# Block 0's attention head sums through DRAM, a later output projection, and block 1's sums behind LN2

## The chip, the cores and the metric

The kernel runs on one core of one Trainium2 chip. The metric is the device time of one execution in microseconds (us); the median of several executions is quoted. One profiled execution gives the trace, whose span is about 2 us shorter than that time. Every variant was run beside the kernel before, on the same chip in the same rounds. Where two variants are compared with each other, they can be from different rounds; the medians of the kernel before differ by at most 0.4 us between rounds (1617.8 to 1618.2).

## The reference

Two transformer layer pairs, A then B, applied twice to x of 2048 tokens by 1024 features in bf16. A is a sliding-window attention with 32 heads of 32 features, 8 offsets per token at distance 2; B is a gated ReLU MLP of 3584 hidden features.

```python
x = A_x
x = x + _A_ref(_layernorm(x), A_wqkv, A_wo)
x = x + _B_ref(_layernorm(x), B_W_gate, B_W_up, B_W_down)
x = x + _A_ref(_layernorm(x), A_wqkv, A_wo)
x = x + _B_ref(_layernorm(x), B_W_gate, B_W_up, B_W_down)
# _A_ref: logits[h, s, w] = sum over the head's 32 features of q[s] * k[s - 2w], masked where s < 2w,
#         softmax over the 8 offsets w, o = attn @ shifted v, then o @ wo
# _B_ref: (relu(x @ W_gate) * (x @ W_up)) @ W_down
```

## The kernel before

The kernel works in 4 token blocks of 512, twice, as n = 0 to 7. It is one list of timed events (`ev`): every event has a nominal time, and the list is sorted by it. TensorE, VectorE and the SP queue are chained to that order (point 3), and the times only set the order. Four parts matter here.

1. *Attention of a block on VectorE.* `prod_sum_steps` multiplies q by shifted k and sums over eight chunks of features, in two halves of the offsets (h = 0, 1), into a tile `s`. What is left of a head is then spread over four partitions, and those four rows have to be added (the "head sums"). Softmax and P·V (`pv_steps`) follow, the result goes to DRAM and comes back transposed as `oT` for the output projection `wo`.
2. *Head sums.* For block 0 before the change, TensorE adds the four rows by a multiplication with a 0/1 matrix `sel`. For all other blocks the tile goes out to DRAM and comes back regrouped, and VectorE adds.

```python
def head_mm(n):                      # block 0, before
    st["L"] = psum_l.tile([P, W, P], F32, tag="L")
    for wh in range(2):
        for tq in range(TPB):        # 8 matmuls
            mm(st["L"][32*tq:32*tq+32, WH*wh:WH*(wh+1), :], lhsT=sel[:],
               rhs=st["s"][:, tq, WH*wh:WH*(wh+1), :], ...)

def head_sum(n):                     # other blocks
    s4 = att[n].pop("s4")            # loaded back from DRAM by load_s
    u = work.tile([P, DG // 2, W, P], F32, tag="ac", bufs=1)
    dv(nc.vector.tensor_tensor, u[:], s4[:, 0:2], s4[:, 2:4], op=ALU.add)
    dv(nc.vector.tensor_tensor, u[:, 0], u[:, 0], u[:, 1], op=ALU.add)
```

3. *The chains of order.* `dv` puts every VectorE instruction behind the one before, and `sp_dma` does the same for transfers on the SP queue. On ScalarE the exponential of the softmax is put behind the instruction listed before it, but the casts of V are put behind nothing, so later casts can run ahead of it. An instruction that has to wait holds up all that were listed after it on that engine or queue.

```python
def sp_dma(dst, src, transpose=False):
    with tc.issue_after(tail_sp[0]):
        tail_sp[0] = start(dst, src).ins
```

4. *Weights.* They come in slabs of 1 MB through a ring of five buffers, as SP transfers in the same queue. The gate and up weights of the MLP are cut into slabs of four 128-column chunks; "slab 4" holds chunks 16 to 19. The MLP of block 0 starts at `t_gu0` with alternating gate and up groups of 8 matmuls; VectorE multiplies relu(gate) by up into `hT`.

The events around block 0's attention, before (cut):

```python
ahead = 2 * KC + 6                   # q/k groups of blocks 2, 3 ahead of wo of block 0 (22 of 32)
t_wo0 = t_qk2 + GRP * ahead
t_fill = t_wo0 + GRP * KC
t_gu0 = t_fill + GRP * (4 * KC - ahead)
...
ev.append((t_v2 + 5.2 * GRP, lambda: head_mm(0)))
spread(softmax_steps(0), t_v2 + 5.3 * GRP, 0.01)
spread(pv_steps(0), t_pv0, 4.3)
...
sums1 = prod_sum_steps(1)            # 16 steps, about 30 VectorE operations
spread(sums1[:4], t_pv0 + 34.5, 4.5)
spread(sums1[4:6], t_wo0 + 0.5, 2.5)
spread(sums1[6:10], t_fill + 1.4, 4.6)
spread(sums1[10:], t_gu0 + 2.6, 5.4)
...                                  # in the MLP of block 0, at = t_gu0:
ev.append((at + 4.0, store_s(1, 0)))
ev.append((at + 37.5, store_s(1, 1)))
ev.append((at + 40.5, load_s(1)))
```

## Time and profile before

| | before |
|---|---|
| time, median | 1618.2 us |
| span of the profiled run | 1616.1 us |
| TensorE busy / VectorE busy | 99% / 70% |
| TensorE waits in all | 2.6 us, all in the first 11 us |
| granted TensorE clock | 1.000 |
| one group of 8 matmuls (128x512) | 1.727 us from start to start |

TensorE is the limit. First come the page's line of busy times, then, from its part on the chain that ended last, the shares by engine.

```profile
PE 1607.6 (99%) x7584; PEld 786.4 (49%) x7633; DVE 1138.5 (70%) x962; ACT 473.5 (29%) x964; POOL 180.3 (11%) x168
...
PE 99%; issue 0%; DMA 0%; DVE 0%; POOL 0%; ACT 0%; DVEq 0%
```

The page says what is busy, but not how near each stage is to a hole. That has to be read from the timelines. Here is VectorE's timeline of the kernel before, around block 0's attention. Columns: start, duration, engine, line, operation, output<-inputs, count, and in brackets the idle time before it and what ended it.

```profile
100.09 2.29 DVE L106 TENSOR_TENSOR s<-ac,t 128x2048 bf16<-128x2048 f32 x1
103.78 0.27 DVE L106 TENSOR_TENSOR L<-L,maskc 32x112 f32<-32x112 f32 x1 [1.40 <-PE L L132]
104.09 1.23 DVE L106 TENSOR_REDUCE m<-L 128x128 f32<-128x1024 f32 x1
...
111.88 4.50 DVE L106 TENSOR_TENSOR pv<-a,vhm 128x4096 bf16<-128x4096 bf16 x2
```

And here is SP's queue of the same kernel, in the MLP of block 0. The columns are the same; the duration is that of the issue, not of the transfer.

```profile
218.29 0.53 SPq L121 DMA_DIRECT2D q<-q_d  x1
230.40 0.56 SPq L121 DMA_DIRECT2D s_d<-s  x1
...
233.84 2.52 SPq L121 DMA_DIRECT2D s<-s_d  x4
...
237.09 1.67 SPq L121 DMA_DIRECT2D w_u<-in_B_W_up_dram  x1
```

The sums of block 0 end at 102.4; TensorE's head sums are there at 103.8, and P·V begins at 111.9. The sums of block 1 end at 230.4 (VectorE's last of them starts at 228.08 and takes 2.29 us). SP's store of them (`s_d<-s`) was reached at 218.8 and had to wait until then; behind it in the queue stand the loads of the sums and then the up weights of slab 4 (`w_u`, 237.09). These weights took 9.4 us to land, at 246.5, and TensorE's first group with them begins 33 groups after 190.01, at 247.0. Its timeline has wo of block 0, the first gate group and that up group at:

```profile
158.93 13.98 PE L132 MATMUL acc_wo<-w_o,oT 128*128 128x512 bf16 x62
...
190.01 1.89 PE L132 MATMUL acc_g<-xnT_b,w_g 128*128 128x512 bf16 x8
...
246.99 1.89 PE L132 MATMUL acc_u<-xnT_b,w_u 128*128 128x512 bf16 x8
```

### The profile page before, as it was taken

The page shows a single profiled execution, that of the slowest core. Times are in us where ns is not written, and L with a number is a line of the kernel's source. Part 1 is how long each engine was busy: PE and PEld are TensorE (multiplying, and loading weights), DVE is VectorE, ACT ScalarE, POOL GpSimd, SP SyncE. Part 2 cuts the span into 40 slices and gives each one's busy share as a digit, 9 for nine tenths or more (in the row PEclk, how much of TensorE's full clock was granted, in tenths as well). Part 3 has the DMA queues.
Part 4 walks back from the last instruction along what each step waited for, and adds up shares of the span by engine and source line. Part 5 has one row for each costly group of instructions (what it writes and reads, how often), then busy time and mean ns, then how long its engine had stood idle before and what let it go on. Part 6 is the DMA issues. An engine that isn't in the chain of part 4 may idle for free.

```text
span 1616.1 us, 18879 instructions
## 1 busy us (share of the span) xinstructions
PE 1607.6 (99%) x7584; PEld 786.4 (49%) x7633; DVE 1138.5 (70%) x962; ACT 473.5 (29%) x964; POOL 180.3 (11%) x168
## 2 busy tenths in 40 slices
PE   9999999999999999999999999999999999999999
PEld 6646544444444445444454444544445444444444
DVE  5999989996989698929389293893939939311211
ACT  4753312132115313603136031361313311131110
POOL 3400100010003002300053000530005100000000
PEclk9999999999999999999999999999999999999999
DMA  9767857596669666784747847489575884655452
GB/s 308 181 187 247 219 163 255 183 218 203 208 195 227 191 185 208 194 248 145 227 159 203 237 156 226 156 202 255 163 227 155 207 241 157 209 161 177 156 167 67
DMA packets 359064, 317.92 MB, mean 197 GB/s; under 512 B 105024, under 2 KB 332736, under 8 KB 358464
## 3 DMA queue, kind: packets, MB, share of 16 engines
q1 hardware_dynamic: 358272, 315.87, 67.1%
q8 instruction: 59, 0.97, 0.3%
q10 hardware_dynamic: 704, 0.85, 0.2%
q14 instruction: 29, 0.24, 0.0%
HBM read 266.29 MB, written 34.66 MB: 186 GB/s over the span
## 4 chain that ended last, share of the span: by engine, by line
PE 99%; issue 0%; DMA 0%; DVE 0%; POOL 0%; ACT 0%; DVEq 0%
PE acc_u L132 24%; PE acc_g L132 24%; PE dacc L132 18%; PE acc_v L132 7%; PE acc_k L132 7%; PE acc_q L132 7%; PE acc_wo L132 7%; PE dacc_pair L132 6%; DMA x<-in_A_x_dram 0%; PE tp_pair L384 0%; DVE bst L103 0%; DVE bst L106 0%; POOL rstd L327 0%; PE L L132 0%; DVE x L838 0%
## 5 line engine op out<-in xcount | busy, mean ns | idle before, releaser
L132 PE MATMUL acc_u<-xnT_b,w_u 128*128 128x512 bf16 x1792 | 423.3, 379 | 0.0
L132 PE MATMUL acc_g<-xnT_b,w_g 128*128 128x512 bf16 x1792 | 423.3, 379 | 0.0
L791 ACT ACTIVATE r<-acc_g 128x512 bf16<-128x512 f32 x224 | 133.6, 596 | 727.5 <-PE acc_g L132 696.8
L106 DVE TENSOR_TENSOR hT<-acc_u,r 128x512 bf16<-128x512 f32 x224 | 150.6, 685 | 241.2 <-PE acc_u L132 238.5
L132 PE MATMUL dacc<-w_d,hT 128*128 128x512 bf16 (+1 forms) x1372 | 300.4, 375 | 1.5
L132 PEld LDWEIGHTS <-hT 128*128 128x128 bf16 x1820 | 178.0, 98 | 209.0
L132 PEld LDWEIGHTS <-w_u 128*128 128x128 bf16 x1792 | 175.3, 98 | 211.4
L132 PEld LDWEIGHTS <-w_g 128*128 128x128 bf16 x1792 | 175.4, 98 | 211.4
L106 DVE TENSOR_TENSOR pv<-a,vhm 128x4096 bf16<-128x4096 bf16 x64 | 143.5, 2282 | 0.0
L838 DVE TENSOR_TENSOR x<-dacc,x 128x512 bf16<-128x512 f32 (+1 forms) x38 | 24.5, 672 | 154.2 <-PE dacc L132 154.2
L606 DVE TENSOR_TENSOR t<-q,k 128x2048 f32<-128x2048 bf16 x56 | 128.0, 2292 | 6.7 <-ACT k L541 4.6
L106 DVE TENSOR_TENSOR t<-q,k 128x2048 f32<-128x2048 bf16 x56 | 127.4, 2285 | 3.7 <-ACT k L541 2.6
L106 DVE TENSOR_TENSOR pv<-pv 128x1024 bf16<-128x1024 bf16 (+1 forms) x128 | 113.7, 949 | 0.0
L547 POOL COPY kh<-k 128x14 bf16<-128x14 bf16 x40 | 56.0, 1406 | 504.2 <-ACT k L541 504.2
L132 PE MATMUL acc_wo<-w_o,oT 128*128 128x512 bf16 x498 | 111.1, 379 | 0.7
L622 DVE TENSOR_TENSOR ac<-ac,t 128x2048 f32<-128x2048 f32 x48 | 109.6, 2284 | 0.3
L106 DVE TENSOR_TENSOR ac<-ac,t 128x2048 f32<-128x2048 f32 x48 | 109.6, 2283 | 0.0
L263 POOL TENSOR_TENSOR st_b<-st_b,neg_half 128x1 f32<-128x1 f32 x29 | 43.9, 1521 | 525.8 <-ACT st_b L262 525.8
L132 PE MATMUL dacc_pair<-w_d,hT 128*128 128x512 bf16 x413 | 95.5, 379 | 0.4
L132 PEld LDWEIGHTS <-oT 128*128 128x128 bf16 x512 | 50.2, 98 | 60.3
L258 ACT ACTIVATE xn_b<-x 128x1024 bf16<-128x1024 bf16 x29 | 30.3, 1045 | 129.3 <-DVE x L106 67.1
L444 ACT CAST vT<-acc_v 128x512 bf16<-128x512 f32 x56 | 32.6, 585 | 57.0 <-PE acc_v L132 56.1
(134 smaller groups left out, 1227.2 us busy)
## 6 DMA issues: line engine op xcount, KB each, us to landing
w_g<-in_B_W_gate_dram SPq DMA_DIRECT2D x56, 1024.0 KB, 7.1
w_u<-in_B_W_up_dram SPq DMA_DIRECT2D x56, 1024.0 KB, 5.4
w_d<-in_B_W_down_dram SPq DMA_DIRECT2D x48, 1024.0 KB, 5.9
w_o<-in_A_wo_dram SPq DMA_DIRECT2D x16, 1024.0 KB, 8.2
vhm<-v_d SPq DMA_DIRECT2D x32, 284.0 KB, 6.7
v_d<-vT SPq DMA_DIRECT2D x8, 1024.0 KB, 9.7
oT<-o_d SPq DMA_DIRECT2D x32, 256.0 KB, 3.4
w_d<-in_B_W_down_dram SPq DMA_DIRECT2D x16, 512.0 KB, 3.9
```

Source lines behind the costliest of these rows:

```text
L106: tail_dve[0] = f(*args, **kwargs).ins
L132: tail_pe[0] = nc.tensor.matmul(*args, **kwargs).ins
L258: nc.scalar.activation(xn, xt[:], ACT.Square, accum_out=sq)
L263: nc.gpsimd.tensor_tensor(rstd, vpe, neg_half[:, 0:1], op=ALU.pow)
L444: tail_act[0] = nc.scalar.copy(st["vT"][:, c, :], acc[:]).ins
L547: nc.gpsimd.tensor_copy(khalo[n][:, c, :], k[:, BLK:BLK + HALO])
L606: nc.vector.tensor_tensor(t[:], i0, i1, op=ALU.mult)
L622: nc.vector.tensor_tensor(o, i0, i1, op=ALU.add)
L791: tail_act[0] = nc.scalar.activation(rs[j][:], acc[:], ACT.Relu).ins
L838: run = dv if n < NB - 2 else (lambda f, *args, **kwargs: f(*args, **kwargs))
```

## The change

Its intent: take block 0's head sums off the busiest engine as in the other blocks, and make room for the longer way: wo of block 0 comes two groups later, and block 1's sums no longer stand between wo's results and LN2. The diff, cut to its core:

```diff
-    sel = const.tile([P, H], BF16, name="sel")        # and its construction, and head_mm
-    def load_s(n):
+    def load_s(n, w0=0, w1=W):                         # a range of offsets
+            s4 = work.tile([P, DG, w1 - w0, P], BF16, tag="t", ...)
-    def head_sum(n):
+    def head_sum(n, w0=0, w1=W):
+        lo, hi = (st["u"][:, i, w0:w1, :] for i in range(2))
+        dv(nc.vector.tensor_tensor, st["u"][:, :, w0:w1, :], s4[:, 0:2], s4[:, 2:4], op=ALU.add)
+        dv(nc.vector.tensor_tensor, lo, lo, hi, op=ALU.add)
         def shift():
-            Lt = st["L"][:] if n == 0 else head_sum(n)
+            if n == 0:
+                head_sum(n, 0, WH)
+                head_sum(n, WH, W)
+            else:
+                head_sum(n)
+            Lt = st.pop("u")[:, 0]
-    ahead = 2 * KC + 6
+    ahead = 3 * KC
+    ev.append((t_sum0 + 4.4 * KC + 1.5, store_s(0, 0)))
+    ev.append((t_sum0 + 4.4 * (2 * KC - 1) + 0.1, store_s(0, 1)))
+    ev.append((t_sum0 + 4.4 * (2 * KC - 1) + 0.2, load_s(0, 0, WH)))
+    ev.append((t_sum0 + 4.4 * (2 * KC - 1) + 0.3, load_s(0, WH, W)))
-    ev.append((t_v2 + 5.2 * GRP, lambda: head_mm(0)))
-    t_pv0 = t_v2 + 4.2 * GRP + 10.0
+    t_pv0 = t_v2 + 4.2 * GRP + 15.0
-    spread(sums1[:4], t_pv0 + 34.5, 4.5)
-    spread(sums1[4:6], t_wo0 + 0.5, 2.5)
-    spread(sums1[6:10], t_fill + 1.4, 4.6)
-    spread(sums1[10:], t_gu0 + 2.6, 5.4)
+    spread(sums1[:4], t_pv0 + 34.5, 3.2)
+    spread(sums1[4:9], t_fill + 3.3, 3.0)
+    spread(sums1[9:], t_gu0 + 2.6, 5.4)
```

Below, part 1 is the way through DRAM, part 2 the later wo (`ahead`), part 3 the new order of `sums1`.

## The prediction

> **What bounds the kernel now.** TensorE. The chain of waits is 99% PE; the list of waits shows PE waiting 2.6 us in all, within the first 11 us. PE's timeline has no gap from 17 us on: 8 matmuls every 1.727 us. So the change can gain only what it takes off PE, and loses every new hole it opens.
>
> **Removed.** The 8 head-sum matmuls. In the timeline they push the next group from 103.03 (by the 1.727 us pitch) to 103.66: -0.63 us. wo of block 0 only changes places with two k groups.
>
> **Added, on VectorE.** Block 0's sums end at 102.38; its softmax started at 103.78. Now: store of the second half (block 1's took 3.4 us; here 1 MB of V is still leaving), four loads issued 0.45 us apart, each landing in 2.7 to 4 us: there at about 110.5. Then 1.9 us of adds (scaled from block 1's 2.28 + 1.22), and the maximum from SBUF costs 1.90 instead of 1.23 from PSUM. P·V starts about 121 instead of 111.88: VectorE is 9 to 10 us late, with almost no idle time until 230 to absorb it.
>
> **Critical path, step by step.**
> 1. wo of block 0 starts at 161.8. P·V ends about 155.5, store 2.3, first load 2.7: oT just in time; hole 0 to 1 us.
> 2. LN2 of block 0 has no sums in its middle any more, so its transposes land by about 187: no hole before the first gate group.
> 3. Those sums now stand ahead of the first gate product: 11 operations x 2.24 us after LN2's end (182.5) put it at 207 instead of 201.2. With six accumulators and three r buffers, gate j must finish before up-group j+4. Hole of 2 to 4 us near 205.
> 4. The largest: the second half of block 1's sums ends about 241.5 instead of 230.37 (9.3 chain, 0.6 LN2 wait, two more gate products ahead). The store of those sums blocks the SP queue until then (waits of SP: 11.6 us for s), and behind it come the s loads and the up-weights of slab 4. Before, that weight load was issued at 237.09 and landed at 246.5; PE needs it at 190.01 + 33 x 1.727 = 247.0: slack 0.5 us. It lands 16.1 us after the sums end, so now at about 257.6. PE is then 10.6 us late in all, step 3 included.
> 5. After it VectorE and PE are both about 11 us late, so their distance is as before: no further hole.
>
> The Trainium skill, "DMA: Bandwidth & Descriptors", section on the anatomy of one DMA, says that a semaphore wait is served by the issuing sequencer before dispatch, not by the DMA engines. This trace agrees: SP issues nothing between 218.8 and 230.4 us. So an unrelated weight load suffers.
>
> **Predicted:** 1618.0 + 10.6 = 1628.6 us; 80% range 1620.5 to 1635. Chances: faster by over 2% 0.01, within 2% 0.97, slower 0.02.
>
> **What would show it.** Step 1: P·V from about 121, PE waiting under 1 us for oT. Step 3: PE waits for hT near 205. Step 4: SP waiting about 20 us for s until 241.5; PE idle 6 to 10 us near 250, ended by a DMA of w_u. Step 5: no PE wait over 1 us after 260. Removed matmuls: groups after 103 are 0.63 us earlier.
>
> **What would make it wrong.** If the half loads land by 107, the hole of step 4 shrinks us for us. If the weight load, issued later, lands faster than 9.4 us, the hole is up to 4 us smaller. If PSUM buffers are assigned otherwise, step 3 grows, but step 4 swallows that. If all holes close, the time is 1617.4.

## The result

The changed kernel took 1639.0 us (1638.0 to 1639.5, four runs) against 1618.2 us of the kernel before in the same rounds: ratio 1.0128, interval 1.011 to 1.0145. It is slower by 20.8 us, within the 2% that counts as the same, but far outside the noise. The profiled run took 1638.0 us, the fastest of the four, so its trace holds about 1 us less than the medians say.

The changed kernel's page has the same outline, with PE at 91% of the chain instead of 99% (the page's busy line, then the chain's shares by engine), although busy time on PE is again 99%:

```profile
PE 1612.0 (99%) x7576; PEld 787.1 (48%) x7625; DVE 1143.4 (70%) x966; ACT 473.1 (29%) x964; POOL 178.0 (11%) x165
...
PE 91%; DVE 5%; DMA 2%; issue 1%; SPq 0%; POOL 0%; ACT 0%; DVEq 0%; POOLq 0%
```

The list of TensorE's waits of the changed kernel shows three that were not there (columns: line that waited <- releaser: us in total, times, longest). Before, the list held none of these lines, only waits of 1.5, 0.8 and 0.3 us at the start of the program.

```profile
PE acc_u L132 <- DMA w_u<-in_B_W_up_dram: 7.0, 1, 7.0
PE acc_wo L132 <- DMA oT<-o_d: 6.5, 1, 6.5
PE acc_g L132 <- DMA xnT_b<-xn_b: 2.5, 1, 2.5
```

TensorE's timeline of the changed kernel, at those places. The bracket at the end is the idle time before the group and what ended it; the duration of a run of matmuls shows their pace.

```profile
148.08 13.98 PE L132 MATMUL acc_k<-xnT_a,w_qk_k 128*128 128x512 bf16 x64
168.56 0.61 PE L132 MATMUL acc_wo<-w_o,oT 128*128 128x512 bf16 x1 [6.50 <-DMA oT<-o_d]
169.38 15.33 PE L132 MATMUL acc_wo<-w_o,oT 128*128 128x512 bf16 x61 [0.22 <-issue]
184.55 13.98 PE L132 MATMUL acc_k<-xnT_a,w_qk_k 128*128 128x512 bf16 x64
200.98 1.89 PE L132 MATMUL acc_g<-xnT_b,w_g 128*128 128x512 bf16 x8 [2.46 <-DMA xnT_b<-xn_b]
...
265.56 3.37 PE L132 MATMUL acc_u<-xnT_b,w_u 128*128 128x512 bf16 x8 [7.00 <-DMA w_u<-in_B_W_up_dram]
268.76 1.89 PE L132 MATMUL acc_g<-xnT_b,w_g 128*128 128x512 bf16 x8
```

The groups have a pitch of 1.727 us, so each line says how late TensorE became. Eight groups after 148.08 would end at 161.89, and wo starts at 168.56. It takes 15.99 us to 184.55 instead of 13.81. The gate groups start at 200.98 instead of 198.36. At 265.56 instead of 257.97 (33 groups after 200.98) comes the first up group of slab 4, and that group of 8 takes 3.20 us instead of 1.73.

| where | TensorE later by |
|---|---|
| start of the program (51.39 against 51.22) | +0.2 |
| head-sum matmuls gone (120.45 against 120.94, less the 0.2) | -0.65 |
| wait for oT before wo of block 0 | +6.7 |
| wo itself, slow | +2.2 |
| wait before the first gate group | +2.6 |
| up to and before the up weights of slab 4 (7.16, and twice 0.2 on the way) | +7.6 |
| the group after it, slow | +1.5 |
| sum (20.05 before the rows are rounded) | +20.1 |

From there on nothing is added: wo of block 1 starts at 330.92 against 310.87, which is 20.05 us. The spans differ by 20.2.

The two slow stretches are the clock. The view by stretches of the changed kernel, over the 4 us after the first hole and the 3 us after the last (columns: stretch, its length, busy time and count for each engine, then the granted clock, DMA share and GB/s):

```profile
168.50:172.50 4.00, 3.73 (x9) 1.47 (x11) 3.96 (x3) 0.01 (x1) 0.00 (x0) 0.50 0.98 309
265.50:268.50 3.00, 2.94 (x7) 1.04 (x8) 2.97 (x4) 0.00 (x0) 0.00 (x0) 0.50 1.10 349
```

In both, the clock is 0.50. After the hole of 2.5 us before the gate groups it stayed at 1.00 (200.9 to 202.8). Before, it was 1.00 in every stretch looked at.

VectorE's timeline of the changed kernel, from the end of block 0's sums to P·V:

```profile
100.24 2.29 DVE L106 TENSOR_TENSOR s<-ac,t 128x2048 bf16<-128x2048 f32 x1
109.99 1.22 DVE L106 TENSOR_TENSOR u<-s 128x1024 f32<-128x1024 bf16 x1 [7.46 <-DMA s<-s_d]
...
113.17 1.23 DVE L106 TENSOR_TENSOR u<-s 128x1024 f32<-128x1024 bf16 x1 [1.23 <-DMA s<-s_d]
...
115.45 1.92 DVE L106 TENSOR_REDUCE m<-u 128x128 f32<-128x1024 f32 x1
...
122.23 1.96 DVE L106 TENSOR_REDUCE ssum<-d 128x128 f32<-128x1024 f32 x1 [3.60 <-ACT d L658]
...
126.47 4.50 DVE L106 TENSOR_TENSOR pv<-a,vhm 128x4096 bf16<-128x4096 bf16 x2
```

P·V starts at 126.5 instead of 111.9: 7.5 and 1.2 us of waiting for the two halves (1.4 us for TensorE before), 3.6 us of waiting for the exponential (1.1 before), and the adds (the maximum alone took 1.92 us instead of 1.23). And SP's timeline, for the line that ended slab 4's hole:

```profile
229.70 0.53 SPq L121 DMA_DIRECT2D q<-q_d  x1
249.09 0.56 SPq L121 DMA_DIRECT2D s_d<-s  x1
...
254.33 2.52 SPq L121 DMA_DIRECT2D s<-s_d  x4
...
257.57 0.39 SPq L121 DMA_DIRECT2D w_u<-in_B_W_up_dram  x1
```

The store of block 1's sums held SP from 230.2 to 249.1 (the list of SP's waits: 18.8 us for `s`, 11.6 before), and the up weights behind it went out at 257.6 instead of 237.1. They landed 7.9 us later, at 265.5, and TensorE began.

### The profile page after: what moved, and what is told of

Read it like the earlier page. It is cut to its first block, busy times and chain, and to the rows that moved or that the text cites. A ratio compares the mean times of both kernels' runs of the same rounds, so it can differ in the third digit from the quotient of the medians. Undisturbed runs are those within 1.5% of the kernel's fastest.

```text
span 1636.3 us, 18874 instructions
## 1 busy us (share of the span) xinstructions
PE 1612.0 (99%) x7576; PEld 787.1 (48%) x7625; DVE 1143.4 (70%) x966; ACT 473.1 (29%) x964; POOL 178.0 (11%) x165
## 4 chain that ended last, share of the span: by engine, by line
PE 91%; DVE 5%; DMA 2%; issue 1%; SPq 0%; POOL 0%; ACT 0%; DVEq 0%; POOLq 0%
PE acc_u L132 22%; PE acc_g L132 22%; PE dacc L132 18%; PE acc_v L132 7%; PE acc_wo L132 6%; PE dacc_pair L132 6%; PE acc_k L132 5%; PE acc_q L132 5%; DVE pv L106 2%; DVE t L106 1%; DVE ac L106 1%; DMA w_g<-in_B_W_gate_dram 1%; DMA w_u<-in_B_W_up_dram 0%; DMA s_d<-s 0%; DMA o_d<-ohm 0%
## 5 line engine op out<-in xcount | busy, mean ns | idle before, releaser
L132 PE MATMUL acc_wo<-w_o,oT 128*128 128x512 bf16 x498 | 113.1, 384 | 7.4 <-DMA oT<-o_d 6.5
L106 DVE TENSOR_TENSOR pv<-pv 128x1024 bf16<-128x1024 bf16 (+1 forms) x128 | 113.6, 948 | 0.0
```

The lines of the kernel that those rows point to most:

```text
L106: tail_dve[0] = f(*args, **kwargs).ins
L132: tail_pe[0] = nc.tensor.matmul(*args, **kwargs).ins
```

## The experiments

The theory after the result: the change makes VectorE late in two ways that both end in the same place. Part 1 adds a round trip to the chain of block 0 (sums, softmax, P·V, oT). Part 3 takes work from VectorE at a time when it could do it. Either makes block 1's sums late, and SP, stuck on their store, makes the weights late (theory B). The rivals: only the round trip counts (A); only the new order counts (C); the added VectorE work, not the waiting, counts (D).

### Undoing part 1, and taking away the round trip alone

`e1_matmul_sums` is the changed kernel with `head_mm(0)` back.

```diff
-    ev.append((..., store_s(0, 0)))  # and store_s(0, 1), load_s(0, 0, WH), load_s(0, WH, W)
+    ev.append((t_v2 + 5.2 * GRP, lambda: head_mm(0)))
```

> The changed kernel, with block 0's head sums back on TensorE as before (wo two groups later and the new order of block 1's sums stay). Theory A, the DRAM round trip alone is the cause: P*V of block 0 starts near 112, no hole, 1618 us. Theory B, round trip and new order each cost: P*V near 112, no wait for oT, but VectorE now idles while wo runs and block 1's sums still end about 60 us after LN2's end, near 241; a hole of some 2.6 us before the first gate group and 7 to 8 us before the up-weights of slab 4, plus 1.5 us of half clock after it: 1628 to 1631 us. Theory C, the new order is all of it: 1637 us or more.

Measured: 1630.4 us (before in these rounds: 1618.15; ratio 1.0074). P·V began at 111.6 and TensorE never waited for oT. The hole at slab 4 was 5.1 us, not the 7 to 8 expected; the total was in the range all the same, with a slow group after the 2.3 us hole before the gate groups as well, which the expectation did not have. These two lines of its TensorE waits stand for what was left:

```profile
PE acc_u L132 <- DMA w_u<-in_B_W_up_dram: 5.1, 1, 5.1
PE acc_g L132 <- ACT kst L538: 2.3, 1, 2.3
```

The second line names a cast of k, which ended at 192.0. The last transpose of LN2's result landed at the same moment (192.1), and before the change the gate groups began (190.01) while such a cast was still to come (190.25), so it is read here as the wait for the transposes; the trace alone doesn't decide it.

Block 1's sums ended at 240.4, as theory B had it. Theory A and theory C fall: part 1 costs some 8.6 us on top of the others (20.8 less 12.3), and 12.3 us remain without it.

`e2_no_round_trip` keeps all of part 1's VectorE work but reads `s` in place instead of its regrouped copy. Its output is wrong, which doesn't matter for the time.

```diff
-        s4 = st.pop(("s4", w0))
+        s4 = st["s"][:, :, w0:w1, :] if n == 0 else st.pop(("s4", w0))
-    ev.append((..., store_s(0, 0)))  # and store_s(0, 1), load_s(0, 0, WH), load_s(0, WH, W)
```

> Wrong result on purpose: the head sums read the products' sums in place instead of their regrouped copy from DRAM, so all VectorE work of the change stays and only the store, the loads and the wait for them go. Theory A/B, waiting is what costs on the chain: P*V starts at 115 to 118 instead of 126.5, no wait for oT. Theory D, the added VectorE work costs: P*V stays at 122 or later. Total under A about 1619 us, under B (new order costs too) 1627 to 1630 us, under D 1635 us or more.

Measured: 1630.7 us (1618.15; 1.0079), 0.7 above the range of theory B and far from that of theory D. P·V began at 115.0, so the added work is worth 3 us of the 14.6 on this chain, and the waiting (for the transfers and for the exponential) 11.5 us. The total equals that of `e1_matmul_sums`: those 3 us were absorbed. Theory D falls.

### Parts 2 and 3 on their own, and all other combinations

`e8_order_alone` and `e9_wo_late_alone` apply one part to the kernel before.

```diff
# e8_order_alone: only the sums1 lines of the diff above
# e9_wo_late_alone:
-    ahead = 2 * KC + 6
+    ahead = 3 * KC
```

> The kernel before, with block 1's sums behind LN2 of block 0 and nothing else. Theory B: VectorE has nothing to do while wo's matmuls run, LN2 ends near 177.6, the sums 59.7 us after it, near 237 instead of 230.4; the up-weights of slab 4 land 16.4 us after that, near 253.7, where TensorE wants them at 247.0: one hole of 6 to 7 us and 1.5 us of half clock, 1625 to 1627 us. Theory A (only the round trip costs): 1618 us.

Measured: 1626.1 us (before 1617.86; 1.0049), with block 1's sums ending at 238.0. VectorE's timeline of this run shows why the "protected" LN2 makes them late:

```profile
160.85 0.69 DVE L106 TENSOR_TENSOR x<-acc_wo,x 128x512 bf16<-128x512 f32 x1 [1.32 <-PE acc_wo L132]
163.38 0.69 DVE L106 TENSOR_TENSOR x<-acc_wo,x 128x512 bf16<-128x512 f32 x1 [1.83 <-PE acc_wo L132]
165.10 0.69 DVE L106 TENSOR_TENSOR x<-acc_wo,x 128x512 bf16<-128x512 f32 x1 [1.03 <-PE acc_wo L132]
...
178.34 2.29 DVE L106 TENSOR_TENSOR t<-q,k 128x2048 f32<-128x2048 bf16 x1
```

VectorE adds wo's results as they come, one per 1.73 us, and idles 1.0 to 1.8 us before each. Before, it spent this time on two more steps of block 1's sums and then found four results ready at once (one line of 2.48 us, x4, at 168.49). The time that VectorE gave away here was not got back before block 1's sums were due.

> The kernel before, with wo of block 0 two groups later and nothing else. It takes 3.45 us from the time between the end of wo and the first gate group (17.3 to 13.8 us), while VectorE runs as before. Theory B: VectorE had been ready in time before, so a hole of 0 to 2 us before the first gate group, all else as before: 1618 to 1620 us. If the shorter time for LN2 were a main cause: 1621 us or more.

Measured: 1620.1 us (1617.86; 1.0013, interval 0.9996 to 1.0029, so not clear of no change). The trace, of the slowest of its four runs (1621.6; the others took 1619.8 to 1620.3), has a hole of 2.8 us before the first gate group, more than the 0 to 2 expected of that hole, though the time lies at the edge of the range. The list of waits again names a cast of k (ended 193.2); the last transpose landed at 193.3. So in this trace the later wo was not free: LN2 had 13.8 us instead of its 17.3.

The remaining combinations, with the changed kernel as the base: `e6_dram_alone` has the old `ahead` and the old order, `e5_sums_before_ln2` only the old order (both with the first four sum steps spaced 3.0 instead of 4.5, which leaves their order as it was), `e4_wo_early` only the old `ahead`.

```diff
# e6_dram_alone: both edits; e5_sums_before_ln2: the second; e4_wo_early: the first
-    ahead = 3 * KC
+    ahead = 2 * KC + 6

-    spread(sums1[:4], t_pv0 + 34.5, 3.2)      # and the next two lines
+    spread(sums1[:4], t_pv0 + 34.5, 3.0)
+    spread(sums1[4:6], t_wo0 + 0.5, 2.5)
+    spread(sums1[6:10], t_fill + 1.4, 4.6)
+    spread(sums1[10:], t_gu0 + 2.6, 5.4)
```

> The changed kernel without its two helpers: head sums through DRAM, but wo of block 0 and the order of block 1's sums as before (only the nominal spacing of the first four sums is tightened, which keeps their order). Theory B: wait for oT of some 10 us plus 2.2 us of half clock, then a wait of some 3 us inside wo because its additions stand behind ten sum operations; the sums of block 1 end near 245, so the up-weights come just in time: 1632 to 1634 us. If the helpers help: 1640 us or more. If the round trip cost only what it added on VectorE's chain (14.6 us) less the slack before wo (6.7 us): 1626 us.

> The changed kernel with the old order of block 1's sums. Theory B: holes of 6.7 us (oT) and 2 to 3 us (bank inside wo), 2.2 us of half clock, 3 us before the first gate group; block 1's sums end near 245, four us earlier than in the changed kernel, so no hole at slab 4 is left: 1631 to 1634 us. If the order does not matter once the round trip is there: 1639 us.

> The changed kernel with wo of block 0 at its old place, two groups earlier. Theory B: VectorE's chain is as in the changed kernel, so oT comes at the same moment and TensorE waits 3.5 us longer for it, 10 us in all; the end of wo does not move; the two groups that now stand after wo close the hole before the first gate group, and block 1's sums end as late as before (249), so the hole at slab 4 stays: 1638 to 1640 us, the same total from other holes. If the later wo bought time: 1642 us or more.

Measured: 1634.1, 1632.8 (before 1617.86) and 1636.1 us (before 1617.77). The first two are as expected (the first 0.1 above its range). In both, the weights of slab 4 came in time, so part 1 without part 3 loses its time elsewhere: for oT, and inside wo, where a bank waits for VectorE. For `e6_dram_alone` the list of TensorE's waits has:

```profile
PE acc_wo L132 <- DMA oT<-o_d: 9.2, 1, 9.2
PE acc_wo L132 <- DVE x L106: 4.1, 1, 4.1
```

The third is 2 us below its range: the hole at slab 4 was 5.0 us, not 7, as block 1's sums ended 1.0 us earlier (248.1) and their store landed in 3.5 us instead of 5.2; why the store was faster was not tested. All eight combinations, as medians less the median before in the same rounds:

| through DRAM | wo later | new order | run | us slower |
|---|---|---|---|---|
| - | - | - | before | 0 |
| - | yes | - | e9_wo_late_alone | 2.2 |
| - | - | yes | e8_order_alone | 8.2 |
| - | yes | yes | e1_matmul_sums | 12.3 |
| yes | - | - | e6_dram_alone | 16.3 |
| yes | yes | - | e5_sums_before_ln2 | 15.0 |
| yes | - | yes | e4_wo_early | 18.3 |
| yes | yes | yes | changed kernel | 20.8 |

No part gains, and the parts don't add up (2.2 + 8.2 + 16.3 = 26.7, against 20.8). Theory B, as it stood, was too simple for part 1: late sums of block 1 end in a hole at slab 4 only with the new order; with the old one TensorE is already late from wo by then. In the runs with that hole the up group starts 15 to 17 us after the sums' end, so what makes VectorE late earlier counts mainly through it. The later wo does help a little (1.3 us) where it was needed, with the DRAM way and the old order; with the new order it costs 2.5 us.

### The queue

`e3_weights_first` moves only the store and the load of block 1's second half behind the weights of slabs 4 and 5 in the SP order.

```diff
-            ev.append((at + 37.5, store_s(1, 1)))
-            ev.append((at + 40.5, load_s(1)))
+            ev.append((at + 43.0, store_s(1, 1)))
+            ev.append((at + 46.0, load_s(1)))
```

> The changed kernel, with the store and load of block 1's second half sums placed behind the up- and gate-weights of slabs 4 and 5 in the SP queue. If head-of-line blocking makes the 7 us hole: that hole is gone with its slow start, 1.5 us, and the holes before wo and before the first gate group stay: 1630 to 1631 us. If the weights are late for another reason (DMA bandwidth, a busy slot): hole as before, 1639 us. If VectorE simply is too late: the hole moves to a wait for hT or to wo of block 1, above 1634 us.

Measured: 1633.9 us (1618.15; 1.0096). The up weights went out at 240.8 instead of 257.6, although block 1's sums were no earlier (248.6), and the hole and its slow group were gone. So the weights were late because of their place in the queue. The time is 3 us above the range: VectorE's lateness, which the hole had hidden, came out in small waits further on, of which these three lines of TensorE's waits tell:

```profile
PE acc_u L132 <- DVE hT L106: 2.2, 2, 1.2
...
PE acc_g L132 <- DVE hT L106: 1.1, 1, 1.1
PE acc_wo L132 <- DVE x L106: 1.0, 1, 1.0
```

### The clock

`e7_warm` fills the two large holes with dummy matmuls into an unused accumulator.

```diff
+    ev.append((t_wo0 - 0.01, lambda: scratch(28)))
     place(wo_steps(0), t_wo0)
+            ev.append((at + 2 * GRP * 16 - 0.01, lambda: scratch(32)))
             ev.append((at + 4.0, store_s(1, 0)))
```

> The changed kernel with 28 dummy matmuls before wo of block 0 and 32 before the gate group ahead of the up-weights of slab 4, about as long as the two holes at full clock, so that TensorE does not idle there. If the half clock after the holes is a cost of its own: granted clock 1.00 throughout, 2.2 us less at wo and 1.5 us less at slab 4, 1635 to 1636 us. If it is not: 1639 us or, as the dummies may overshoot, up to 1640 us.

Measured: 1634.9 us (1618.15; 1.0103), mean granted clock 1.0. wo of block 0 took its full-speed time again (first the dummies, from TensorE's timeline of this run):

```profile
162.15 6.21 PE L132 MATMUL scratch<-ones 128*128 128x512 bf16 x28
```

Then wo itself, from the same timeline:

```profile
169.09 13.99 PE L132 MATMUL acc_wo<-w_o,oT 128*128 128x512 bf16 x64 [0.73 <-DMA oT<-o_d]
```

64 matmuls of wo in 13.99 us, where the changed kernel needed over 15.9 us, and the first up group of slab 4 ran at full speed too. So the slow clock after a hole is a cost of its own. The medians fall by 4.1 us, but that is not its clean size: the two traced runs are only 2.6 us apart, the store of block 1's sums landed in 3.5 us instead of 5.2 in this trace, which nothing here explains, and the 32 dummies ran on for about 1 us beyond the weights' landing (263.3, the up group began at 264.5).

### What the round trip is made of

`e11_exp_before_cast` puts the exponential ahead of one cast in ScalarE's order, `e10_first_half_early` loads the first half of the sums earlier (with one staging buffer less, for room); in the trace its loads went out at 90.7 instead of 103.2, which is 12.5 us and not the 20 of the expectation.

```diff
# e11_exp_before_cast
-                tail_act[0] = nc.scalar.copy(st["vT"][:, c, :], acc[:]).ins
+                with (tc.issue_after(tail_exp[0]) if (n, c) == (3, KC - 1) else nullcontext()):
+                    tail_act[0] = nc.scalar.copy(st["vT"][:, c, :], acc[:]).ins
# e10_first_half_early
-    ev.append((t_sum0 + 4.4 * (2 * KC - 1) + 0.2, load_s(0, 0, WH)))
+    ev.append((t_sum0 + 4.4 * KC + 18.0, load_s(0, 0, WH)))
```

> The changed kernel with the exponential of block 0 placed before the last cast of block 3's V in ScalarE's order instead of behind it. In the changed kernel its input was ready at 118.6 and it began at 121.1, because that cast stood first and waited for TensorE. If queue order is the reason: it begins near 119.5, P*V near 124.8 instead of 126.5, and each us gained on this chain comes back once in the total, as every later step hangs on it: 1637 to 1638 us. If ScalarE is simply slow to start: no change, 1639 us.

> The changed kernel with the first half of the sums loaded back some 20 us earlier, so that only the second half is on the chain (one staging buffer less, to make room). The second half then lands near 110.5 instead of 113.1. If that wait were what sets P*V: 2.5 us less, 1636.5 us. If the exponential's place behind the casts sets it, as I now think: P*V stays at 126.4 and the wait only moves to ScalarE, 1638 to 1639.5 us.

Measured: 1635.8 and 1638.8 us (before 1617.77). In the changed kernel the exponential's input was ready at 118.6, and ScalarE did this (its timeline):

```profile
120.65 0.58 ACT L438 CAST vT<-acc_v 128x512 bf16<-128x512 f32 x1 [1.14 <-PE acc_v L132]
121.14 1.06 ACT L658 ACTIVATE d<-d 128x1024 f32<-128x1024 f32 x1
```

The cast at 120.65 had to wait for TensorE, and the exponential stood behind it, although the list has the exponential behind the sixth of the 16 V groups of blocks 2 and 3 and this cast belongs to the sixteenth. The Trainium skill, "PSUM — Partial Sum Buffer", section on engine and sequencer instructions, says that the queues of ScalarE, VectorE and GpSimd are strictly first in, first out; this trace agrees, and in `e11_exp_before_cast`, where the order is turned, the exponential ran at 119.1 and P·V at 124.4, 2.0 us earlier:

```profile
119.09 1.06 ACT L659 ACTIVATE d<-d 128x1024 f32<-128x1024 f32 x1
```

Against the kernel before in the same rounds the loss fell by 2.9 us (20.8 to 18.0), more than the 1 to 2 expected; in the trace the output store behind P·V also landed a little sooner (4.2 instead of 5.0 us).

`e10_first_half_early` met its expected time but not its reason: the second half landed at 113.6, no earlier at all. The store of it took 6.3 us, ending 0.9 us after a store of 1 MB of V that had been issued 1.5 us before it. `e13_v_store_behind` puts that store of V behind the sums' transfers and the exponential ahead of the last three casts.

```diff
-    ev.append((t_v2 + 3.0, store_v(1)))
+    ev.append((t_sum0 + 4.4 * (2 * KC - 1) + 0.35, store_v(1)))
```

> The changed kernel with the store of block 1's V put behind the store and loads of block 0's sums in the SP queue, and the exponential ahead of the last three casts so that ScalarE does not hide the gain. If sharing the DMA engines with V's store stretched the round trip: the second store lands 3.5 to 4 us after its issue instead of 5.5, the second half near 111 instead of 113.1, P*V begins near 122 instead of 126.5, total 1632 to 1635 us. If not: second half still near 113, P*V near 124.5, 1636 us.

Measured: 1633.1 us (before 1618.1; 1.0098). The store landed after 3.6 us instead of 5.5, the second half at 111.4, P·V began at 122.2, all as expected. The Trainium skill, "DMA: Bandwidth & Descriptors", section "Issuing engines are not separate DMA queues", says that DMAs run on the same 16 DMA engines and interleave, whichever engine started them. Both stores here are SP's; the run shows what sharing means, that a large store nobody waits for can stretch a small one that everybody waits for (5.5 us beside it, 3.6 without it), and not whether the two interleave or follow each other. Of its four runs two took 1631.2 and 1631.3 at a mean clock of 0.998 and two 1634.9 and 1635.6 at 0.995. The traced one is the fastest, and in it the holes of 2.6 us before wo and 2.3 us before the gate groups left the clock alone; that one of them lets it fall in the slower pair is a guess, as those have no trace.

### Repairs together

`e12_three_repairs` combines the early first half, the exponential ahead of three casts and the weights first; `e14_and_weights_first` is `e13_v_store_behind` with the weights first (the edits are those shown).

> First half early, the exponential ahead of the last three casts of V, and the weights of slabs 4 and 5 ahead of the store of block 1's sums, all in one. If the chain and the SP order explain the loss: P*V near 122, a wait of 0 to 2 us for oT without half clock, 1 to 3 us before the first gate group, no wait for the weights, small waits for hT: 1621 to 1626 us. Anything above 1630 us would mean that something is missing from the account.

Measured: 1630.5 us (1617.77; 1.0077), above its range and above the 1630 that by its own words would mean something missing. It relied on the second half landing near 110.5, and it landed at 113.9, because the store of V was still in the way; P·V began at 124.7 and TensorE waited 4.9 us for oT, at half clock after it.

> As the run before, and the weights of slabs 4 and 5 ahead of the store of block 1's sums. If the account is complete, what is left is some 2 us of wait for oT, 2.5 us before the first gate group, and 3 us of later waits for hT and x as seen with the weights first alone: 1623 to 1628 us. Far above means that a term is missing.

Measured: 1626.9 us (1618.1; 1.0055), in the range, at a clock of 1.0. What is left (the list of TensorE's waits of this run) is 1.8 us for oT, 1.4 us before the gate groups, and small waits for VectorE:

```profile
PE acc_u L132 <- DVE hT L106: 2.3, 2, 1.3
PE acc_wo L132 <- DMA oT<-o_d: 1.8, 1, 1.8
PE acc_g L132 <- DVE hT L106: 1.6, 1, 1.6
...
PE acc_g L132 <- DMA xnT_b<-xn_b: 1.4, 1, 1.4
PE acc_wo L132 <- DVE x L106: 1.0, 1, 1.0
```

These and the 0.65 us gained make 7.4 us, against a measured 8.8; the rest is not accounted for. No version beat the kernel before. That none can was not shown; but the prize is 0.65 us, and the new order alone costs 8.2 us (`e8_order_alone`); the later wo alone costs 2.2 us, which is not clear of no change (`e9_wo_late_alone`).

## Why the prediction was wrong

The direction, the place and the mechanism of the largest loss were right, the size was half: 1628.6 predicted, 1620.5 to 1635 as the range, 1639.0 measured. Point by point:

| step, as the prediction put it | predicted | measured |
|---|---|---|
| head-sum matmuls removed | -0.63 | -0.65 |
| second half of the sums there | 110.5 | 113.1 |
| P·V starts | 121 (9 to 10 late) | 126.5 (14.6 late) |
| LN2 of block 0 ends on VectorE | 182.5 | 189.5 |
| 1: wait for oT | 0 to 1 | 6.7 |
| half clock after the holes | not in the sum | 3.7 |
| 2: from LN2's end to its last transpose landed | 4.5 | 11.3 |
| 2: before the first gate group | 0 | 2.6 |
| 3: wait for hT near 205 | 2 to 4 | 0.4 |
| 4: block 1's sums end | 241.5 | 249.1 |
| 4: weights land after the sums' end | 16.1 | 16.4 |
| 5: further holes | none | none |

- **Where the miss lies.** Once TensorE has to wait for the weights of slab 4, their landing decides how late it is in all, and the holes before it count only as far as they delay VectorE. Predicted was a landing at 257.6, 10.6 us late. The up group began at 265.56, 18.6 us late, and ran 1.5 us slow: 20.05 us. The 9.4 us of difference are 7.6 for the end of block 1's sums, 0.3 for the way from there to the landing, and 1.5 for the clock. The sums end 59.6 us after LN2 (59.0 predicted), also in `e1_matmul_sums` and `e8_order_alone`, so the term to look for is LN2's end, 7.0 us late: 5.5 us of it is P·V's start, and most of the rest is VectorE waiting for a late wo (0.8 and 1.0 us in its timeline).
- **The term that failed is "Added, on VectorE": P·V at 121, measured 126.5.** The wait for the exponential was carried over from before, 1.1 us, and was 3.6: its input was ready at 118.6, but ScalarE's order left it behind the last cast of V, until 121.1. Turning that order alone brings P·V to 124.4 (`e11_exp_before_cast`). The second half of the sums landed 2.6 us late as well, but in the changed kernel that was hidden: as the exponential waited for the cast, a landing at the predicted 110.5 would not have moved P·V. This is an estimate from the times above and was not run, as `e10_first_half_early` brought no earlier landing. With both mended P·V comes at 122.2 (`e13_v_store_behind`): from the end of the sums to the landing it takes 9.1 us instead of 10.6, so V's store accounts for 1.5 of the 2.6 us, and the rest stays open. The adds were about right (3 us in `e2_no_round_trip`, the slower maximum included).
- **Step 1 failed with it.** "oT just in time" had 1.3 us of slack by its own numbers (155.5 + 2.3 + 2.7 against 161.8). P·V ended 5.3 us later than put there (160.8), and the store of the output took 5.0 us, not the 2.3 us of before: 5.3 + 2.7 - 1.3 is the hole of 6.7. The trace shows the store issued behind 2 MB of weights at 154.6 and 155.3 and landing while the DMA engines were fully busy; that these slowed it was not tested.
- **Step 2 failed.** VectorE was done with LN2 4.9 us after wo's end (6.9 foreseen), but the transposes of its result did not go out at once: the first was issued right behind 2 MB of weights and took 10.1 us to land, and the last went out at 197.0, 7.5 us after VectorE was done. The window had shrunk from 17.3 to 13.8 us, and in `e9_wo_late_alone` this alone goes with a hole of 2.8 us. Here the prediction read only VectorE's part of the path.
- **Step 3** was milder than said (0.2 us twice, at 215.0 and 225.6, each right behind a product for hT), presumably because steps 1 and 2 had already made TensorE late by 11 us.
- **Step 4 was right in every relation.** The slack of 0.5 us, the stuck queue (18.8 us against "about 20") and the 16 us from sums to weights hold; its input, the end of the sums, was 7.6 us off because LN2's end was. As `e3_weights_first` shows, taking SP's order away removes the hole. What the prediction did not see is that the new order is a second sufficient cause: in `e8_order_alone`, without any round trip, block 1's sums are late by 7.6 us as well.
- **The clock was left out of the sum.** The Trainium skill, "TensorE: Matmul & The Clock Gate", part 1, says that TensorE falls to half rate after an idle window of about 3.4 us. The trace agrees: 0.50 after the holes of 6.7 and 7.2 us. A prediction that lists holes of 6 to 10 us should have added it: it slowed TensorE by 3.7 us in the trace, of which the 1.5 us behind slab 4 stand in the total as they are.
- **The range** was too narrow. The errors of the exponential, the transfers, the output store and the transposes all have the same sign, as each was taken from a place where less stood in front of it or beside it; only step 3's has the other.

## What to carry to other kernels

Before moving work off the busiest engine, look for the stage with the least slack downstream of the receiving engine: here 0.5 us at a weight load that only shares a queue with the work that was moved. Cost a DRAM round trip on a chain with the transfers that are in flight at that moment, and give every in-order queue on the way (here ScalarE and SP) its own look, for what stands in front. When a hole of several us is predicted on TensorE, add the slow clock after it (here after every hole of 3.9 us and more, and after some of 2.1 to 2.3 us). To protect one step by moving filler work behind it is only free if the engine has something else to do meanwhile.

## What the Trainium skill lacked or had wrong

- "TensorE: Matmul & The Clock Gate" advises to keep gaps under about 3 us. A hole of 2.3 us (`e1_matmul_sums`, before the first gate group) was followed by 8 matmuls in 3.55 us and a clock of 0.53, as this line of its stretches shows; so were holes of 2.2 us in `e5_sums_before_ln2` (3.46 us) and 2.1 us in `e11_exp_before_cast` (3.33 us). The changed kernel's hole of 2.5 us at the same place left the clock at 1.00, and one of 2.8 us in `e9_wo_late_alone` left the group at 1.89 us. Its remark that the window is free-running could make like holes differ, but not a hole shorter than one window slow; the cause stays open, and the stated limit is not safe:

```profile
192.20:194.00 1.80, 1.75 (x5) 0.69 (x6) 1.80 (x1) 0.00 (x0) 0.00 (x0) 0.53 0.58 132
```

- "DMA: Bandwidth & Descriptors" says that a semaphore wait is served by the issuing sequencer, but not what this means for a shared queue: with one store waiting 18.8 us for its data (11.6 before), a weight load with no relation to it went out 20.5 us later (257.6 instead of 237.1), and at 240.8 when it was put ahead of that store (`e3_weights_first`).
- The same page gives about 2 us of fixed cost per DMA, for the path that GpSimd issues, and nothing for a regrouping through DRAM. Here, on SP's queue, 0.5 MB out and 1 MB back (the first half had gone out earlier) took 10.6 us from the end of the sums to the last landing beside a 1 MB store, and 9.1 us with that store behind it (`e13_v_store_behind`).
